# One kernel of attention, gate and routed experts: conversion spread over three engines, unsplit key projections, gathers two units ahead

## Chip, cores, metric

The kernel runs on one core of a Trainium2 chip. The metric is device time in microseconds (us) of one execution, median of several. The engines: PE (TensorE, matmuls), DVE (VectorE), ACT (ScalarE), POOL (GpSimd), SP (SyncE, which issues DMAs here). Each engine works through its own queue in order.

## What is computed

Three stages, one after the other, on 2304 tokens (4 batches of 576), 8 heads of 64, model width 512.

```python
# 1. attention with random features; phi for q and k
proj = einsum('bhsd,df->bhsf', x, w_phi)
proj = proj - max(abs(proj), axis=-1)
phi  = concatenate([exp(proj), exp(-proj)], axis=-1)
kv, z = einsum('bhsf,bhsd->bhfd', k_p, v), sum(k_p, axis=2)
attn = einsum('bhsf,bhfd->bhsd', q_p, kv) / (einsum('bhsf,bhf->bhs', q_p, z) + 1e-6)
# 2. causal convolution of 5 taps as a gate
y = (sigmoid(conv(x, conv_w)) * (x @ w_val)) @ w_out
# 3. per token one of 8 experts: argmax of y @ w_gate,
#    or the one of the token before where sigmoid(y @ w_local) >= 0.5
out[s] = softmax(y @ w_gate)[e] * (relu(y[s] @ w1[e]) @ w2[e])
```

The weights `w_val`, `w_out` and `conv_w` come to the device as 64-bit patterns and are converted to fp32 there.

## The kernel before

The matmuls of weight run in a reduced fp32 format (F32R), three for one product: a number is split into a high part (`hi_of`, a cast) and a low part (`lo_of`, the subtraction), and high x high, high x low and low x high are summed. A full fp32 matmul needs no split.

**Key and query pass** (`run`, L602). 18 tiles of 128 tokens of keys, then 18 of queries, each in two halves of four heads. `load` (L85) brings a raw tile, four buffers; `split` (L104) makes its parts, the cast on ACT and the subtraction on POOL; `proj` (L114) multiplies with the features, with six F32R matmuls for a half tile, or with two fp32 ones where there is no split, as for key tile 0 (L123); DVE then takes the maximum (L131) and subtracts it (L133); ACT makes both exponentials (L136). Three half tiles later `kv` (L147) accumulates keys against values in PSUM, and `kv_done` (L166) copies a batch's sum out. For queries `tq` transposes and `nm` multiplies with that sum.

**Background work.** `from64` (L299) converts a piece of 512 columns of a matrix in six steps: DVE works on the integer pattern (L313, L318, L319, L320, L321, L322), ACT takes an absolute value (L314). Each step is one entry of a queue, `bgq` for the small vector and the four pieces of `w_val`, `bg2` for the four of `w_out`; `setup_w` (L343) adds an entry that begins a piece and one that splits the result, and for `w_out` a fold onto the router's weights. `run` takes 1.3 entries per half tile in the key pass and up to seven in the query pass. A planner that simulates the engines sets the order in which each engine gets its instructions, except where an order is pinned.

**Gate and output.** `conv`, `val` and `lgt_a`/`lgt_b` follow the queries; `ymm` (L522) makes the rows y, 12 F32R matmuls of 512 columns for 128 tokens, and writes them and the expert probabilities to HBM (`y_d`). `yfill(n)` (L412) pins n of these matmuls into PE's queue; the routing (from L675) is a chain of small transposes on PE and steps on DVE, with such fills between, ten of them ahead of the first transpose (L676). After the table (L754) 30 idle matmuls bridge the time until the first rows are gathered (L759).

**Experts.** Ten units: one of two chunks of 128 tokens for each expert, then two of three chunks, whose expert is read at run time. `gather` (L808) fetches rows of y and their probabilities with an indirect DMA of POOL, three buffers; `rows` (L816) transposes and splits them and picks out the probabilities, by a copy (L830) or, in three-chunk units, by three DVE steps (L833 to L835). `unit` (L839) runs the first layer, eight slices of 12 matmuls into `hp` (three buffers), ACT making the high part of the hidden rows (L852) and DVE the remainder `hlo` (L853); then the second layer, chunk by chunk, each scaled by its probability (L867) and scattered by POOL (L868). Behind the first chunk `mid` (L909) calls `rows` for the next unit; that unit's `gather` stands at the beginning of the current one (L899). A loop at the end serves further units; it is empty for these tokens.

Of the kernel before, what the change touches and what calls it, by code (L numbers as in the profile page):

```python
# [8 lines left out]
F32 = mybir.dt.float32  # L9
# [4 lines left out]
AF = mybir.ActivationFunctionType  # L14
# [7 lines left out]
NT = T // 128  # L22
# [7 lines left out]
NCOL = 2 * E + 3 * NUNIT  # L30
YLAG = 4
WARM = 30
FRESH = -1.5 * 2.0 ** -23


@with_exitstack
def body(ctx, tc, qT, kT, v1, wbd, w_val, conv_w, w_out, w_gl, w1, w2, out):
# [65 lines left out]

    def split(nm, t):  # L104

        if t >= NT or (nm, t) in hl_t or (nm, t) == ("k", 0):
            return
        hi = ap.tile([128, 4, 128], F32R, tag="qkh", name="qkh", bufs=2)
        lo = ap.tile([128, 4, 128], F32R, tag="qkl", name="qkl", bufs=2)
        hi_of(A, hi, raw_t[nm, t])  # L110
        lo_of(G, lo, raw_t[nm, t], hi)
        hl_t[nm, t] = (hi, lo)
# [186 lines left out]
    def from64(raw, n, tag):  # L299

        hi = raw[:, :, 1]
        top = raw.bitcast(U16)[:, :, 1]
        if tag == "w":
            slots = (("a", "xh"), ("b", "xh"), ("m", "xl"), ("f", "xl"))
            a, b, m, f = [mp.tile([128, n], I32, tag=w, name=f"t{z}{tag}", bufs=2) for z, w in slots]
        else:
            a, b, m, f = [mp.tile([128, n], I32, tag=f"t{z}{tag}", name=f"t{z}{tag}", bufs=1) for z in "abmf"]
        af, bf, mf, ff = [z.bitcast(F32) for z in (a, b, m, f)]  # L310

        def first():
            V.tensor_scalar(f, hi, 0x07ffffff, 3, op0=ALU.bitwise_and, op1=ALU.logical_shift_left)  # L313
            A.activation(af, hi.bitcast(F32), AF.Abs)  # L314

        return f, [
            first,
            lambda: V.scalar_tensor_tensor(b, hi, -0x40000000, f, ALU.bitwise_and, ALU.bitwise_or),  # L318
            lambda: V.tensor_scalar(m, b, -0x800000, None, op0=ALU.bitwise_and),  # L319
            lambda: V.scalar_tensor_tensor(mf, top, 0.5, mf, ALU.add, ALU.mult),  # L320
            lambda: V.scalar_tensor_tensor(ff, mf, 2.0 ** -36, bf, ALU.mult, ALU.add),  # L321
            lambda: V.scalar_tensor_tensor(ff, af, 2.0 ** -15, ff, ALU.is_ge, ALU.mult),  # L322
        ]

    def setup_small():
        wgl = mp.tile([128, 4, E + 1], F32, name="wgl")
# [85 lines left out]
    def yfill(n):  # L412
        for _ in range(n):
            while rest:
                mm = next(rest[0], None)
                if mm is None:
                    rest.pop(0)
                else:
                    pin(mm)
                    break  # L420
# [252 lines left out]


    tp = pst([NT, 128], "tp1")  # L675
    yfill(10)  # L676
    pin(PE.transpose(tp, rc["code"], ident))
    sc = t_([NT, 128], "sc")
    V.tensor_tensor_scan(sc, rc["onef"][0:NT, :], tp, 0.0, ALU.mult, ALU.max)
# [128 lines left out]
    def gather(gcols):  # L808
        xs = []
        for gc in gcols:  # L810
            xg = fx.tile([128, YW], F32, tag="xg", name="xg", bufs=3)
            G.indirect_dma_start(out=xg, out_offset=None, in_=y_d, in_offset=bass.IndirectOffsetOnAxis(ap=gc, axis=0))
            xs.append(xg)
        return xs

    def rows(xs, probs):  # L816

        xh = fx.tile([128, 4, UNIT], F32R, tag="xh", name="xh")
        xl = fx.tile([128, 4, UNIT], F32R, tag="xl", name="xl")
        pv = []  # L820
        for j, xg in enumerate(xs):
            xp = ps_f.tile([128, 4, 128], F32, tag="xp", name="xp", bufs=2)
            for c in range(4):
                PE.transpose(xp[:, c, :], xg[:, c * 128:(c + 1) * 128], ident)
            sl = slice(j * 128, j * 128 + 128)
            hi_of(A, xh[:, :, sl], xp)
            lo_of(V, xl[:, :, sl], xp, xh[:, :, sl])
            p = fx.tile([128, 1], F32, tag="p", name="p", bufs=6)
            if isinstance(probs, int):
                V.tensor_copy(p, xg[:, D + probs:D + probs + 1])  # L830
            else:
                es = fx.tile([128, E], F32, tag="es", name="es")
                V.tensor_scalar(es, io8, probs, None, op0=ALU.is_equal)  # L833
                V.tensor_tensor(es, es, xg[:, D:YW], ALU.mult)
                V.tensor_reduce(p, es, axis=AX.X, op=ALU.add)  # L835
            pv.append(p)
        return xh, xl, pv

    def unit(hl, x, scols, between, mid):  # L839
        (w1h, w1l), (w2h, w2l) = hl  # L840
        xh, xl, pv = x
        n = len(pv) * 128
        hh = fx.tile([128, 8, UNIT], F32R, tag="hh", name="hh", bufs=1)
        hlo = fx.tile([128, 8, UNIT], F32R, tag="hlo", name="hlo", bufs=1)
        for f in range(8):
            hp = ps_f.tile([128, UNIT], F32, tag="hp", name="hp", bufs=3)
            i = 0
            for k in range(4):
                for wt, xt in ((w1h, xh), (w1l, xh), (w1h, xl)):
                    PE.matmul(hp[:, 0:n], lhsT=wt[:, k, f * 128:(f + 1) * 128], rhs=xt[:, k, 0:n], start=(i == 0), stop=(i == 11))  # L850
                    i += 1
            A.activation(hh[:, f, 0:n], hp[:, 0:n], AF.Relu)  # L852
            V.scalar_tensor_tensor(hlo[:, f, 0:n], hp[:, 0:n], 0.0, hh[:, f, 0:n].bitcast(F32), ALU.max, ALU.subtract)  # L853
            if f % 2 == 1:
                between()
        for j in range(len(pv)):
            op = ps_f.tile([128, 512], F32, tag="op", name="op", bufs=2)
            sl = slice(j * 128, j * 128 + 128)
            i = 0
            for f in range(8):  # L860
                for ht, wt in ((hh, w2h), (hh, w2l), (hlo, w2h)):
                    PE.matmul(op, lhsT=ht[:, f, sl], rhs=wt[:, f, :], start=(i == 0), stop=(i == 23))  # L862
                    i += 1
                if f in (3, 7):
                    between()
            osb = fx.tile([128, 512], F32, tag="osb", name="osb")
            A.activation(osb, op, AF.Copy, scale=pv[j])  # L867
            G.indirect_dma_start(out=out, out_offset=bass.IndirectOffsetOnAxis(ap=scols[j], axis=0), in_=osb, in_offset=None,  # L868
                                 bounds_check=T - 1, oob_is_err=False)
            if j == 0:  # L870
                mid()
# [18 lines left out]
            p()()  # L890
    xs = gather(cols(gidx, units[0][0], units[0][1]))
    cur_x = rows(xs, unit_probs(0))
    for i, (c0, n, e) in enumerate(units):
        last = i + 1 == len(units)
        nxt = {}
        work = []
        if not last:
            nxt["w"], pieces = unit_weights(i + 1)
            nxt["xs"] = gather(cols(gidx, units[i + 1][0], units[i + 1][1]))  # L899
            started = [p() for p in pieces[:3]]  # L900
            todo = pieces[3:]

# [5 lines left out]

        def mid():  # L909
            if not last:  # L910
                nxt["x"] = rows(nxt["xs"], unit_probs(i + 1))

        unit(cur_w, cur_x, cols(sidx, c0, n), between, mid)
        while not last and started:
# [47 lines left out]
```

## Time and profile before

| | us |
|---|---|
| runs of the kernel | 601.49, 601.50, 603.31 (median 601.5) |
| the profiled execution | 600.88, of which the span from first to last instruction 599.2 |
| PE busy | 565.9 (94%) |
| DVE busy | 373.3 (62%) |
| ACT busy | 314.3 (52%) |
| POOL busy | 231.4 (39%) |

Busy time is the union of an engine's instructions; a matmul's end is modelled, so a short pause between matmuls can vanish in it. "Idle before" an instruction is the time in which its engine had nothing running, with the instruction or DMA that ended it. Rows of a time line give the start, the length, engine, line, operation and operands of an instruction or of several alike.

### The profile page before, as it was taken

How to read it: one execution, taken by the hardware profiler on the slowest of the kernel's cores; microseconds unless marked ns; L12 is line 12 of the kernel's file. 1: busy time of each engine (PE TensorE's matmuls, PEld its weight loads, DVE VectorE, ACT ScalarE, POOL GpSimd, SP SyncE). 2: the span in 40 equal slices, each digit the busy share in tenths (PEclk: the TensorE clock that was granted, in tenths of full speed). 3: DMA queues.
4: the chain of work that ended last, by engine and by line, in shares of the span. 5: the costliest groups of instructions: out<-in, count | busy, mean ns of one | idle time of the engine just before them, and what ended most of it. 6: DMA issues, size and time to landing. Idle time of an engine off the chain costs nothing. (4 is left out here: it accounts for less than half of the span.)

```text
span 599.2 us, 13671 instructions
## 1 busy us (share of the span) xinstructions
PE 565.9 (94%) x5545; PEld 497.4 (83%) x5546; DVE 373.3 (62%) x744; ACT 314.3 (52%) x581; POOL 231.4 (39%) x257
## 2 busy tenths in 40 slices
PE   7997998999999999998998999999998989999993
PEld 6886987889888988886775888988987879898982
DVE  6999859688877877478504766666554746460110
ACT  5767855665766655555215565564553646441210
POOL 4454323489878876472204102302302123011001
PEclk9999999999999999999998999999999999999997
DMA  8933422101110001034226877866866648520000
GB/s 278 339 101 124 131 74 59 49 2 37 36 38 2 21 19 38 19 124 139 111 107 200 288 237 254 268 181 189 284 186 203 203 137 276 179 90 35 18 18 35
DMA packets 46017, 76.82 MB, mean 128 GB/s; under 512 B 3839, under 2 KB 22399, under 8 KB 45952
## 3 DMA queue, kind: packets, MB, share of 16 engines
q1 hardware_dynamic: 39840, 60.55, 32.5%
q0 software_dynamic: 3520, 10.58, 4.9%
q10 hardware_dynamic: 2592, 4.79, 2.1%
q8 instruction: 45, 0.74, 0.5%
q14 instruction: 20, 0.16, 0.1%
HBM read 66.39 MB, written 10.56 MB: 128 GB/s over the span
## 5 line engine op out<-in xcount | busy, mean ns | idle before, releaser
L868 POOL DMA_INDIRECT out<-osb,sidx x22 | 28.6, 1302 | 206.7 <-ACT osb L867 161.4
L850 PE MATMUL hp<-xh,w1h 128*128 128x256 f32 (+1 forms) x320 | 94.6, 296 | 7.3 <-DVE hlo L853 5.8
L850 PE MATMUL hp<-xh,w1l 128*128 128x256 f32 (+1 forms) x320 | 94.2, 294 | 0.0
L850 PE MATMUL hp<-xl,w1h 128*128 128x256 f32 (+1 forms) x320 | 93.8, 294 | 0.0
L850 PEld LDWEIGHTS hp<-xh,w1h 128*128 128x128 f32 x320 | 60.8, 190 | 10.4 <-DVE hlo L853 7.1
L862 PE MATMUL op<-w2h,hh 128*128 128x512 f32 x176 | 69.1, 401 | 0.2 <-ACT hh L852 0.2
L51 DVE TENSOR_TENSOR w2l<-wraw,w2h 128x1024 fp32r<-128x1024 f32 x40 | 48.9, 1224 | 32.1 <-ACT w2h L48 22.4
L51 POOL TENSOR_TENSOR qkl<-raw,qkh 128x512 fp32r<-128x512 f32 x35 | 46.7, 1334 | 55.5 <-ACT qkh L48 55.4
L862 PE MATMUL op<-w2l,hh 128*128 128x512 f32 x176 | 67.9, 395 | 0.0
L862 PE MATMUL op<-w2h,hlo 128*128 128x512 f32 x176 | 66.8, 395 | 0.0
L51 DVE TENSOR_TENSOR w1l<-wraw,w1h 128x1024 fp32r<-128x1024 f32 x40 | 48.9, 1250 | 22.6 <-ACT w1h L48 22.6
L131 DVE TENSOR_REDUCE m<-pj 128x4 f32<-128x512 f32 x72 | 49.1, 685 | 22.0 <-PE pj L128 21.9
L265 DVE SCALAR_TENSOR_TENSOR acc<-xT,tfs,acc 128x256 f32<-128x256 f32 (+1 forms) x112 | 53.9, 486 | 13.3 <-ACT acc L263 12.0
L850 PEld LDWEIGHTS hp<-xh,w1l 128*128 128x128 f32 x320 | 60.7, 190 | 1.5
L850 PEld LDWEIGHTS hp<-xl,w1h 128*128 128x128 f32 x320 | 60.5, 189 | 0.0
L48 ACT CAST w2h<-wraw 128x1024 fp32r<-128x1024 f32 x40 | 41.8, 1049 | 34.0 <-DMA wraw<-w 25.2
L853 DVE SCALAR_TENSOR_TENSOR hlo<-hp,hh 128x256 fp32r<-128x256 f32 (+1 forms) x80 | 33.9, 445 | 39.6 <-ACT hh L852 39.5
L852 ACT ACTIVATE hh<-hp 128x256 fp32r<-128x256 f32 (+1 forms) x80 | 31.2, 404 | 48.0 <-PE hp L850 47.6
L48 ACT CAST w1h<-wraw 128x1024 fp32r<-128x1024 f32 x40 | 40.4, 1052 | 29.6 <-DMA wraw<-w 29.6
L133 DVE TENSOR_TENSOR pp<-pj,m 128x512 f32<-128x512 f32 x72 | 48.8, 683 | 2.5 <-PE tp L185 0.8
L158 PE MATMUL kv<-v,ex 128*64 128x65 f32 (+1 forms) x1280 | 46.9, 224 | 3.3 <-DVE kvsb L170 1.4
L158 PEld LDWEIGHTS kv<-v,ex 128*64 128x64 f32 (+1 forms) x1280 | 41.0, 137 | 9.3 <-DVE kvsb L170 1.7
(192 smaller groups left out, 1364.5 us busy)
## 6 DMA issues: line engine op xcount, KB each, us to landing
wraw<-w SPq DMA_DIRECT2D x80, 512.0 KB, 4.5
v<-v SPq DMA_DIRECT2D x18, 260.0 KB, 3.2
y_d<-ysb ACTq DMA_DIRECT2D x18, 260.0 KB, 2.0
raw<-qT SPq DMA_DIRECT2D x18, 256.0 KB, 3.4
raw<-kT SPq DMA_DIRECT2D x17, 256.0 KB, 5.0
wr<-w_val SPq DMA_DIRECT2D x4, 512.0 KB, 7.4
wr<-w_out SPq DMA_DIRECT2D x4, 512.0 KB, 7.6
xg<-y_d,gidx POOLq DMA_INDIRECT x22, 5.4
```

What stands on the lines that cost most here:

```text
L48: (A.copy if eng is A else eng.tensor_copy)(hi, src)
L51: eng.tensor_tensor(lo, src, hi.bitcast(F32), ALU.subtract)
L131: V.tensor_reduce(m, pj, axis=AX.X, op=ALU.max, apply_absolute_value=True)
L133: V.tensor_tensor(pp, pj, m.unsqueeze(2).to_broadcast([128, 4, 128]), ALU.subtract)
L158: PE.matmul(kv_ps[b][blk // 7][mh * 64:mh * 64 + 64, (blk % 7) * VW:(blk % 7 + 1) * VW], lhsT=kp_t[t, hh][off:off + n, sg, h, mh * 64:mh * ...
L265: W["tap"] = V.scalar_tensor_tensor(acc[c], xs, cw[:, kk, c:c + 1], acc[c], ALU.mult, ALU.add)
L850: PE.matmul(hp[:, 0:n], lhsT=wt[:, k, f * 128:(f + 1) * 128], rhs=xt[:, k, 0:n], start=(i == 0), stop=(i == 11))
L852: A.activation(hh[:, f, 0:n], hp[:, 0:n], AF.Relu)
L853: V.scalar_tensor_tensor(hlo[:, f, 0:n], hp[:, 0:n], 0.0, hh[:, f, 0:n].bitcast(F32), ALU.max, ALU.subtract)
L862: PE.matmul(op, lhsT=ht[:, f, sl], rhs=wt[:, f, :], start=(i == 0), stop=(i == 23))
L868: G.indirect_dma_start(out=out, out_offset=bass.IndirectOffsetOnAxis(ap=scols[j], axis=0), in_=osb, in_offset=None, bounds_check=T - 1, oo ...
```

## The change

Four edits. Key tiles are no longer split, and so all go through the fp32 matmuls. The conversion of a piece has four steps in place of six; one operation goes to ACT (a copy with scale and bias, which reads the upper half-word) and two to POOL (a multiplication and an addition), and DVE keeps four. The first fill of the routing has 18 matmuls instead of 10. Gathers have six buffers and are issued two units ahead, in `mid`; the probabilities are taken in `unit`, behind the last remainder of the first layer on DVE.

```diff
+XG = 6
     def split(nm, t):
-        if t >= NT or (nm, t) in hl_t or (nm, t) == ("k", 0):
+        if t >= NT or (nm, t) in hl_t or nm == "k":
             return
...
-        def first():
+        def high():
             V.tensor_scalar(f, hi, 0x07ffffff, 3, op0=ALU.bitwise_and, op1=ALU.logical_shift_left)
             A.activation(af, hi.bitcast(F32), AF.Abs)
-        return f, [
-            first,
-            lambda: V.scalar_tensor_tensor(b, hi, -0x40000000, f, ALU.bitwise_and, ALU.bitwise_or),
-            lambda: V.tensor_scalar(m, b, -0x800000, None, op0=ALU.bitwise_and),
-            lambda: V.scalar_tensor_tensor(mf, top, 0.5, mf, ALU.add, ALU.mult),
-            lambda: V.scalar_tensor_tensor(ff, mf, 2.0 ** -36, bf, ALU.mult, ALU.add),
-            lambda: V.scalar_tensor_tensor(ff, af, 2.0 ** -15, ff, ALU.is_ge, ALU.mult),
-        ]
+        def join():
+            V.scalar_tensor_tensor(b, hi, -0x40000000, f, ALU.bitwise_and, ALU.bitwise_or)
+            A.activation(ff, top, AF.Copy, bias=2.0 ** -37, scale=2.0 ** -36)
+        def low():
+            V.tensor_scalar(m, b, -0x800000, None, op0=ALU.bitwise_and)
+            G.tensor_tensor(mf, ff, mf, ALU.mult)
+            G.tensor_tensor(ff, mf, bf, ALU.add)
+        return f, [high, join, low, lambda: V.scalar_tensor_tensor(ff, af, 2.0 ** -15, ff, ALU.is_ge, ALU.mult)]
...
-    yfill(10)
+    yfill(18)
     pin(PE.transpose(tp, rc["code"], ident))
...
-            xg = fx.tile([128, YW], F32, tag="xg", name="xg", bufs=3)
+            xg = fx.tile([128, YW], F32, tag="xg", name="xg", bufs=XG)
...
-            p = fx.tile([128, 1], F32, tag="p", name="p", bufs=6)
-            if isinstance(probs, int):
-                V.tensor_copy(p, xg[:, D + probs:D + probs + 1])
-            else:
...
-            pv.append(p)
+            pv.append((xg, probs))
+    def prob(xg, probs):
+        p = fx.tile([128, 1], F32, tag="p", name="p", bufs=6)
+        if isinstance(probs, int):
+            V.tensor_copy(p, xg[:, D + probs:D + probs + 1])
+        else:
...
+        return p
...
-            V.scalar_tensor_tensor(hlo[:, f, 0:n], hp[:, 0:n], 0.0, hh[:, f, 0:n].bitcast(F32), ALU.max, ALU.subtract)
+            low = V.scalar_tensor_tensor(hlo[:, f, 0:n], hp[:, 0:n], 0.0, hh[:, f, 0:n].bitcast(F32), ALU.max, ALU.subtract)
             if f % 2 == 1:
                 between()
+        with tc.issue_after(low.ins):
+            pv = [prob(*z) for z in pv]
...
     cur_x = rows(xs, unit_probs(0))
+    xs = {1: gather(cols(gidx, units[1][0], units[1][1]))}
     for i, (c0, n, e) in enumerate(units):
...
-            nxt["xs"] = gather(cols(gidx, units[i + 1][0], units[i + 1][1]))
...
         def mid():
             if not last:
-                nxt["x"] = rows(nxt["xs"], unit_probs(i + 1))
+                nxt["x"] = rows(xs.pop(i + 1), unit_probs(i + 1))
+                if i + 2 < len(units):
+                    xs[i + 2] = gather(cols(gidx, units[i + 2][0], units[i + 2][1]))
```

## Rows read from the trace of the kernel before

**Rows 1.** By stage: from:to, length; PE, PEld, DVE, ACT, POOL; clock, DMA, GB/s.

```profile
20.00:62.00 42.00, 38.13 (x725) 33.33 (x725) 41.34 (x67) 30.58 (x58) 19.66 (x14) 1.00 0.48 157
62.00:91.40 29.40, 29.40 (x590) 26.37 (x586) 19.90 (x30) 19.39 (x37) 9.00 (x7) 1.00 0.35 104
91.40:115.00 23.60, 20.04 (x273) 18.05 (x273) 21.83 (x47) 15.80 (x32) 11.08 (x8) 1.00 0.18 51
115.00:250.00 135.00, 133.77 (x1733) 119.55 (x1731) 98.79 (x250) 82.24 (x187) 102.34 (x119) 1.00 0.08 25
...
452.00:492.00 40.00, 35.02 (x228) 31.61 (x227) 20.82 (x37) 17.81 (x30) 9.55 (x7) 1.00 0.57 181
```

**Rows 2.** Time line of PE, steady key pass: start, length, instruction, count, idle before.

```profile
82.58 0.38 PE L128 MATMUL pj<-wb_hi,qkh 128*128 128x256 f32 x1
82.80 0.28 PE L128 MATMUL pj<-wb_lo,qkh 128*128 128x256 f32 x1
82.92 0.28 PE L128 MATMUL pj<-wb_hi,qkl 128*128 128x256 f32 x1
...
84.57 0.39 PE L128 MATMUL pj<-wb_hi,qkh 128*128 128x256 f32 x1
```

**Rows 3.** Time line of PE at the start: key tile 0 unsplit, then tile 1.

```profile
3.62 3.75 PE L128 MATMUL pj<-wraw,raw 128*128 128x256 f32 x8 [3.62 <-DMA raw<-kT]
...
7.61 0.42 PE L128 MATMUL pj<-wb_hi,qkh 128*128 128x256 f32 x1
7.83 0.41 PE L128 MATMUL pj<-wb_lo,qkh 128*128 128x256 f32 x1
```

**Rows 4.** Groups by line and form: busy us, mean ns; idle before, by whom ended.

```profile
L51 POOL TENSOR_TENSOR qkl<-raw,qkh 128x512 fp32r<-128x512 f32 x35 | 46.7, 1334 | 55.5 <-ACT qkh L48 55.4
...
L320 DVE SCALAR_TENSOR_TENSOR tmw<-wr,tmw 128x512 f32<-128x512 uint16 x8 | 6.8, 855 | 0.0
...
L321 DVE SCALAR_TENSOR_TENSOR tfw<-tmw,tbw 128x512 f32<-128x512 f32 x8 | 5.4, 678 | 0.0
...
L314 ACT ACTIVATE taw<-wr 128x512 f32<-128x512 f32 x8 | 5.4, 671 | 2.1 <-DVE tfw L321 2.1
...
L128 PE MATMUL pj<-wraw,raw 128*128 128x256 f32 x8 | 3.8, 651 | 3.6 <-DMA raw<-kT 3.6
```

**Rows 5.** Time line of PE: last output matmuls and the idle ones, 512 columns.

```profile
311.38 0.39 PE L532 MATMUL yps<-wout_l,gh 128*128 128x512 f32 x1
311.61 0.40 PE L532 MATMUL yps<-wout_h,gl 128*128 128x512 f32 x1
...
312.50 6.64 PE L759 MATMUL idle<-ohl,ones 128*128 128x512 bf16 x29
```

**Rows 6.** Time line of DVE in the key pass.

```profile
23.85 0.68 DVE L133 TENSOR_TENSOR pp<-pj,m 128x512 f32<-128x512 f32 x1
24.45 0.41 DVE L319 TENSOR_SCALAR tmw<-tbw 128x512 int32<-128x512 int32 x1
...
41.61 1.49 DVE L319 TENSOR_SCALAR tmw<-tbw 128x512 int32<-128x512 int32 x1 [0.48 <-POOL wval_l L51]
```

**Rows 7.** Time line of PE: its longest waits from 20 to 62 and 91.4 to 115.

```profile
55.11 1.27 PE L158 MATMUL kv<-v,ex 128*64 128x65 f32 x36 [1.16 <-DVE kvsb L170]
...
102.61 1.15 PE L197 MATMUL num<-kvsb,ex 128*64 128x65 f32 x32 [1.18 <-ACT ex L139]
```

**Rows 8.** Time line of PE: first transpose of the routing.

```profile
282.33 0.28 PE L677 MATMUL tp<-ident,code 128*18 128x128 f32 x1 [1.69 <-DVE code L520]
```

**Rows 9.** Time line of DVE in the last two-chunk unit.

```profile
459.98 0.17 DVE L834 TENSOR_TENSOR es<-es,xg 128x8 f32<-128x8 f32 x1 [4.03 <-DMA xg<-y_d,gidx]
...
461.36 1.08 DVE L853 SCALAR_TENSOR_TENSOR hlo<-hp,hh 128x256 fp32r<-128x256 f32 x3
```

**Rows 10.** Time line of PE, first layer, the waits behind those of rows 9.

```profile
461.83 0.39 PE L850 MATMUL hp<-xh,w1h 128*128 128x256 f32 x1 [2.66 <-DVE hlo L853]
...
488.23 0.38 PE L850 MATMUL hp<-xh,w1h 128*128 128x256 f32 x1 [2.32 <-DVE hlo L853]
```

More of the change, by code (lines that the diff above doesn't have):

```diff
@@ L827, in rows @@
             lo_of(V, xl[:, :, sl], xp, xh[:, :, sl])
-            p = fx.tile([128, 1], F32, tag="p", name="p", bufs=6)
-            if isinstance(probs, int):
-                V.tensor_copy(p, xg[:, D + probs:D + probs + 1])
-            else:
[L832 to L835, printed above, removed]
-            pv.append(p)
-        return xh, xl, pv
+            pv.append((xg, probs))
+        return xh, xl, pv
+    def prob(xg, probs):
[3 more added lines that the diff above has]
+        else:
+            es = fx.tile([128, E], F32, tag="es", name="es")
+            V.tensor_scalar(es, io8, probs, None, op0=ALU.is_equal)
+            V.tensor_tensor(es, es, xg[:, D:YW], ALU.mult)
+            V.tensor_reduce(p, es, axis=AX.X, op=ALU.add)
+        return p
     def unit(hl, x, scols, between, mid):
```

## Prediction

> **What bounds the kernel now.** I read the table by stages first, because the page's 94% for TensorE (PE) is a mean over stages with different limits. In [rows 1] the second column is PE's busy time. From 62 to 91.4 us and from 115 to 250 us PE is idle for at most 1% of the stretch: there only PE's own work counts, and an engine made faster beside it gains nothing. The exceptions are 20 to 62 us (PE 38.13 of 42.00, VectorE, DVE, 41.34), 91.4 to 115 us (PE 20.04 of 23.60, DVE 21.83) and 452 to 492 us (PE 35.02 of 40.00, and DVE only half busy). In the first two PE waits for a saturated DVE; in the last it waits for something that DVE itself waits for. Second I read PE's timeline for the size of one step of the key pass, third DVE's timeline in the three bad stretches for what ended PE's waits.
>
> **Part 1, raw key projections: more work on PE.** In the steady stretch one half tile of keys takes PE 1.99 us, from the projection at 82.58 to the next at 84.57 [rows 2]: six reduced-precision matmuls of 256 columns, 0.12 us apart, then the kv matmuls. The change replaces the six by two full fp32 matmuls. Tile 0 of the keys already runs so: the eight instructions in [rows 3] are four matmuls, so each is two passes, and a half tile needs four passes. They took 3.75 us together; less the last one's length (their mean is 0.65 [rows 4]), that is 3.1 us for seven starts, 0.44 each, while the reduced ones right after start 0.22 apart, not the 0.12 of later on. So PE still ran at half pace there, and a pass costs twice a reduced matmul of the same columns. At full pace no row has one. Bounds: 0.216 us, the spacing of the 512-column bf16 matmuls (6.64 us, less 0.40 for the last one's length as of the 512-column row above it, over 29 intervals, since 30 were issued and one is missing from the record), and 0.24 us, twice 0.12. The 512-column reduced matmuls beside them stand 0.23 apart [rows 5]. I take 0.224, between the two 512-column rows, the nearest kin in streaming time. A half tile then costs 4 x 0.224 = 0.90 in place of 6 x 0.12 = 0.72, that is 0.18 more; 17 tiles have 34 halves, **+6.1 us** (34 x 0.144 = +4.9 to 34 x 0.24 = +8.2). It lies on the path: PE is the bound in the key pass.
>
> [...]
>
> What goes in return: 17 casts on ScalarE (ACT) and 17 subtractions on GpSimd (POOL), 1.33 us each [rows 4]. Neither is the bound. Loads of raw tiles now wait for the projection and not for the split, with four buffers and loads three tiles ahead: about 12 us of lead at two half tiles of 2 us each. I cost that at nothing; if SyncE's queue stood still behind such a load, the later key and value tiles queued behind it would come late too, and PE would wait.
>
> **Part 2, the conversion of the two weight matrices.** Eight pieces of 512 columns. DVE loses two of its six operations (855 and 678 ns), ACT gains one copy (its Abs of the same size took 671 ns), POOL gains two two-input operations (1.33 us each by its subtraction) [rows 4]. DVE starts one such operation every 0.60 us [rows 6], so the eight pieces give back 16 x 0.60 = 9.6 us of DVE, and up to 12.3 by durations. POOL gets 16 x 1.33 = 21.3 us and loses 17 x 1.33 = 22.6. Fewer steps also mean fewer pops of the background queue: a value piece took 8 and takes 6, an output piece 9 and now 7 with its fold. At 1.3 pops a half tile over 36 half tiles there are some 45: before, 6 + 4 x 8 = 38 went to the small vector and value pieces and 7 were left for the output matrix; after, 4 + 4 x 6 = 28 go there and 17 are left, two and a half output pieces. So most of what DVE converts in the stretch from 91.4 to 115 us moves into the key pass.
>
> What it is worth is PE's idle time in the two DVE-bound stretches. From 20 to 62 us it is 42.00 - 38.13 = 3.87 us [rows 1]; the largest single wait is for DVE's late kvsb copy, 1.16 us at 55.11 [rows 7]. DVE's load per half tile falls to two operations at 0.60 plus some 0.4 of conversion (1.9 us a piece in 4.6 half tiles), well under the 2.17 us that PE will need. Next late is then PE itself, and the swap of the kv accumulators between batches stays. I take **-3.4** (-2.0 to -3.9). From 91.4 to 115 us it is 3.56 us, for instance 1.18 us at 102.61 [rows 7]. With one and a half pieces in place of three the DVE stretch is no longer full; I take **-2.6** (-1.0 to -3.6). PE's transposes and folds of the output pieces move with them and cost the same.
>
> The change adds waits: ACT's copy overwrites what DVE's second operation reads, so ACT waits for DVE; POOL waits for both; DVE's last operation waits for POOL. Behind the last one on DVE stand the reduce and subtract of later half tiles, for which ACT's exponentials and PE's kv wait. This is the first rival.
>
> **Part 3, 18 fills instead of 10 ahead of the first routing transpose.** PE stands idle 1.69 us at 282.33 until DVE's code is there [rows 8]; eight more output matmuls at 0.23 [rows 5] are 1.84 us of work that is needed anyway and stands now behind the routing. They fit the hole: **-1.7** (0 to -1.7). The last output rows, for which the gather waits, then land that much earlier.
>
> **Part 4, gathers two units ahead and probabilities behind the first layer.** At 459.98 DVE sits idle 4.03 us in the middle of a unit: its next instruction multiplies the gathered probabilities, and the gather has not landed. A second such wait follows. Only then the three hidden remainders behind it (hlo, 461.36) are made [rows 9], and PE, which has no free accumulator, resumes at 461.83 after 2.66 us; so again at 488.23 after 2.32 [rows 10]. Both holes belong to the gathers for the two three-chunk units, which had three buffers between them; the row has their probability steps queued ahead of the running unit's remainders. With six buffers and an issue one unit earlier (some 22 us) the rows lie there long before; and the probabilities stand behind the last hlo, so that nothing of that layer is queued behind them. Moved with them: the gathers pass, on POOL's queue, from the start of a unit to behind its first scatter; the scatters of later chunks stand behind them, at about 1 us an issue, and nothing but the end of the program waits for those. In starts instead of idle ends each hole is some 0.15 longer: **-5.3** (-4.0 to -5.5).
>
> **Sum.** The profiled execution took 600.9 us (span 599.2). +6.1 - 3.4 - 2.6 - 1.7 - 5.3 = -6.9, so 594.0; the median of the runs is 0.6 above the profiled one, so **594.6**. All ends against it: +8.2 - 2.0 - 1.0 - 0 - 4.0 = +1.2 (602.7); all for it: +4.9 - 3.9 - 3.6 - 1.7 - 5.5 = -9.8, and about 2 us more from the refill of PE's pipeline after some 15 to 20 short waits: 589.7.
>
> **Rivals.**
> *The round trip over POOL stops DVE (slower).* Place: DVE's last operation of a piece, in the key pass. If it is queued directly behind its own chain, DVE stands for two POOL operations and the ACT copy, 2 x 1.33 + 0.67 = 3.3, with handovers about 3.9 us a piece. A piece comes every 6/1.3 = 4.6 half tiles, 10 us of PE; DVE needs 4.6 x 1.2 = 5.5 for keys and 1.9 for the piece, so the spare is 2.6 us. Above that it decides: 1.3 us too much over seven pieces is 9 us, and the 3.4 of the key pass is not gained. 594.6 + 9 + 3.4 = 607. For it: DVE runs in order and already waited for POOL once, at 41.61 [rows 6]. Against it: key work stands between the conversion's operations there, so the queue need not stop. Chance 0.08.
> *The stall behind the hidden layer keeps its length*, because DVE is late for other reasons (weight remainders of the next unit queue there too): 594.6 + 5.3 = 599.9. Against it: the idle time is DVE's own, and the row names the gather. Chance 0.06.
> *Raw weight loads are not hidden at full pace.* A load of 128 stationary columns fits into the 0.12 us between two reduced matmuls [rows 2], so it is at most that long. If it stood bare before each pass: 4 x 0.12 x 34 = 16 us more, 611. Against it: at half pace the passes of [rows 3] start two reduced spacings apart and no more, which leaves no room for a bare load. Chance 0.03.
> That the longer fill does nothing would give 596.3 and lies inside the range.
>
> **How the numbers follow.** The forecast holds 0.83 with its bounds 589.7 to 602.7, of which little lies above 599.7. The range of 589 to 601 leaves out the first and third rival and the outer ends. A measurement here tells 0.3% (1.8 us) from no change: faster 0.80, same 0.09 (mostly the second rival), slower 0.11.
>
> **What would show it.** Right: in the key pass raw passes 0.22 apart and a steady half tile of 2.15 to 2.2 us; no PE idle above 1 us between 20 and 62 us beyond batch swaps; no wait at the first routing transpose; no wait for a gather on DVE after the first unit, and no PE gap above 1 us around the three-chunk units. Wrong: DVE idle ended by a POOL operation of the conversion; raw passes above 0.25; PE waiting for raw tiles; a hole of two microseconds still before one of the three-chunk units.

## The result, and the profile after

The changed kernel takes **596.9 us** (median; 594.06 to 598.66 in four runs) against 602.4 for the kernel before in the same measurement: a ratio of **0.989**, 95% interval 0.986 to 0.993, or 5.6 us less. The forecast was 594.6 with a range of 589 to 601. The profiled execution took 596.0 us, span 594.2, against 600.9 and 599.2.

The line numbers are some four higher than before. Marks worked out from the two time lines of PE (us): first kv matmul, end of the key pass, first routing transpose, end of the output matmuls, first expert matmul, last matmul's end.

| | kv | keys end | routing | outputs end | experts | end |
|---|---|---|---|---|---|---|
| before | 10.46 | 91.45 | 282.33 | 311.85 | 323.14 | 589.70 |
| after | 12.02 | 94.97 | 285.50 | 313.18 | 325.89 | 584.36 |

So the front half became 1.3 us longer, the handover to the experts another 1.4 longer, and the experts 8.1 shorter (266.56 to 258.47). By stage, to be held against [rows 1] (from:to, length, then busy time of PE, PEld, DVE, ACT, POOL, then clock, DMA share, GB/s):

```profile
20.00:62.00 42.00, 38.96 (x676) 30.62 (x675) 35.37 (x57) 29.93 (x54) 17.75 (x14) 1.00 0.51 148
62.00:94.90 32.90, 32.85 (x586) 26.93 (x584) 25.65 (x37) 21.43 (x39) 12.27 (x9) 1.00 0.35 99
94.90:117.00 22.10, 21.69 (x279) 20.08 (x275) 14.76 (x30) 11.80 (x26) 9.91 (x8) 0.92 0.17 49
117.00:250.00 133.00, 131.73 (x1656) 116.48 (x1656) 99.90 (x251) 81.90 (x183) 102.82 (x120) 1.00 0.10 30
323.00:331.00 8.00, 6.23 (x28) 5.70 (x29) 6.05 (x7) 4.45 (x8) 4.55 (x4) 0.57 0.90 325
452.00:492.00 40.00, 40.00 (x256) 36.15 (x255) 23.44 (x36) 20.69 (x33) 10.79 (x7) 1.00 0.59 191
```

DVE is no longer full in the first of these stretches (35.37 of 42.00, before 41.34) nor in the third (14.76 of 22.10). The hole of the last row is gone: PE is busy for all 40 us. New are the clock column in the third row (0.92) and the fifth row (0.57): stretches at half clock, a granted clock of 0.50. Before, there was one such stretch while PE worked, 3.41 us at the start of the experts (from 323.49). In both traces the clock falls to 0.50 once more behind the last matmul, for the last 6.1 us before and 7.6 after.

PE's time line of the steady key pass, as [rows 2], and of the start, as [rows 3]:

```profile
79.02 1.13 PE L129 MATMUL pj<-wraw,raw 128*128 128x256 f32 x4
80.08 1.15 PE L159 MATMUL kv<-v,ex 128*64 128x65 f32 x32
81.17 0.48 PE L129 MATMUL pj<-wraw,raw 128*128 128x256 f32 x1
...
3.61 8.48 PE L129 MATMUL pj<-wraw,raw 128*128 128x256 f32 x24 [3.61 <-DMA raw<-kT]
```

A half tile is now 2.15 us (79.02 to 81.17), 0.16 more than the 1.99 before. Four passes fill 1.13 us, the last of them 0.48 as the row of one; (1.13 - 0.48) / 3 is **0.216 us** between passes at full pace.

Groups by line and form, the conversion's operations (as [rows 4]), and two of DVE's waits in its time line:

```profile
L326 DVE SCALAR_TENSOR_TENSOR tfw<-taw,tfw 128x512 f32<-128x512 f32 x8 | 6.3, 782 | 5.0 <-POOL tfw L324 5.0
...
L323 POOL TENSOR_TENSOR tmw<-tfw,tmw 128x512 f32<-128x512 f32 x8 | 10.2, 1277 | 34.5 <-DVE tmw L322 28.9 <-ACT ex L139 5.0 <-ACT ex L140 0.6
L324 POOL TENSOR_TENSOR tfw<-tmw,tbw 128x512 f32<-128x512 f32 x8 | 10.2, 1273 | 0.6
...
20.68 0.69 DVE L326 SCALAR_TENSOR_TENSOR tfw<-taw,tfw 128x512 f32<-128x512 f32 x1 [1.42 <-POOL tfw L324]
...
41.85 0.69 DVE L326 SCALAR_TENSOR_TENSOR tfw<-taw,tfw 128x512 f32<-128x512 f32 x1 [1.47 <-POOL tfw L324]
```

So DVE does stand for POOL's round trip, five times, 5.0 us in all, 1.5 at most. PE's own waits of the key pass that are left are the swaps of the batches (time line of PE; [rows 7] before), and the wait of [rows 8] is gone, with an output matmul right behind the transpose:

```profile
32.80 1.03 PE L159 MATMUL kv<-v,ex 64*64 64x65 f32 x28 [0.60 <-ACT kvsb L171]
34.59 1.59 PE L159 MATMUL kv<-v,ex 64*64 64x65 f32 x42 [0.76 <-DVE kvsb L171]
...
54.92 0.34 PE L159 MATMUL kv<-v,ex 128*64 128x65 f32 x4 [0.62 <-DVE kvsb L171]
...
285.26 0.40 PE L535 MATMUL yps<-wout_h,gl 128*128 128x512 f32 x1
285.50 0.27 PE L680 MATMUL tp<-ident,code 128*18 128x128 f32 x1
285.52 0.48 PE L535 MATMUL yps<-wout_h,gh 128*128 128x512 f32 x1
```

The handover to the experts, POOL's and PE's time line:

```profile
318.31 1.20 POOL L815 DMA_INDIRECT xg<-y_d,gidx  x1 [10.23 <-DMA y_d<-ysb]
320.76 0.94 POOL L815 DMA_INDIRECT xg<-y_d,gidx  x1 [1.24 <-PE idle L762]
...
324.10 1.12 PE L827 MATMUL xp<-ident,xg 128*128 128x128 f32 x4 [1.47 <-DMA xg<-y_d,gidx]
325.89 0.58 PE L857 MATMUL hp<-xh,w1h 128*128 128x256 f32 x1 [0.68 <-ACT xh L49]
```

The second gather stands 1.24 us for the idle matmuls: one of the six buffers lies over memory that these still read. PE gets its first expert matmul 5.41 us behind the last idle one, 4.00 before, and the low stretch around it, at a clock of 0.50, lasts 6.83 us (from 323.84) instead of 3.41.

In the experts, the two longest waits of PE that are left, and what ACT did ahead of the second (time lines of PE and ACT; [rows 10] before):

```profile
366.57 0.39 PE L857 MATMUL hp<-xh,w1h 128*128 128x256 f32 x1 [0.77 <-DVE hlo L860]
381.44 0.50 PE L871 MATMUL op<-w2h,hh 128*128 128x512 f32 x1 [0.93 <-ACT hh L859]
...
380.06 1.05 ACT L49 CAST w2h<-wraw 128x1024 fp32r<-128x1024 f32 x1 [3.27 <-DMA wraw<-w]
381.01 0.38 ACT L859 ACTIVATE hh<-hp 128x256 fp32r<-128x256 f32 x1
```

The hidden part `hh` stood in ACT's queue behind a cast of the next unit's weights that waited for its DMA. DVE waits for no gather any more behind the first unit; before that was 14.9 us in six waits.

### The profile page after: what moved, and what is told of

Its sections match the earlier page's. It is cut to its first block, busy times and chain, and to the rows that moved or that the text cites. A ratio compares the mean times of both kernels' runs of the same rounds, so it can differ in the third digit from the quotient of the medians.

```text
span 594.2 us, 13524 instructions
## 1 busy us (share of the span) xinstructions
PE 569.9 (96%) x5477; PEld 495.5 (83%) x5478; DVE 365.2 (61%) x726; ACT 313.1 (53%) x573; POOL 238.0 (40%) x258
## 5 line engine op out<-in xcount | busy, mean ns | idle before, releaser
L815 POOL DMA_INDIRECT xg<-y_d,gidx x22 | 36.7, 1669 | 98.5 <-DVE p L838 83.4
```

## The experiments

Twelve versions, each beside the kernel before. Besides the ratio I use one worked-out number, **full-clock length**: span times mean granted clock, averaged over a version's runs. It is an estimate of what the span would be if PE had been the bound in every stretch at a clock of 0.50 and had had 1.00 there. It takes the clock's part out of a difference, roughly, since waits in these stretches are scaled like work; the stretches behind the last matmul (6.1 and 7.6 us in the two profiles) are in it as well. The profile gives the clock as a share of full speed: where an expectation names a frequency, what was measured is 0.50, and no run shows the frequency. The runs of one version scatter in it by 0.9 to 2.6 us (standard deviation), so that a row of the table holds to 1 to 2 us, and the difference of two rows to about 2. For the kernel before it is 593.0 to 593.5 in the three measurements that list its clocks, for the changed one 585.6, here held against 593.1. Mean clocks are 0.987 and 0.985.

| version | ratio, 95% interval | median us | full-clock, against before |
|---|---|---|---|
| changed kernel | 0.989 [0.986, 0.993] | 596.9 | -7.5 |
| raw_alone | 1.015 [1.012, 1.018] | 611.1 | +4.5 |
| conversion_alone | 1.006 [1.003, 1.009] | 606.1 | +0.1 |
| gathers_alone | 0.989 [0.987, 0.992] | 596.8 | -6.3 |
| gathers_ahead_alone | 0.997 [0.995, 0.999] | 600.2 | -3.3 |
| probabilities_alone | 1.065 [1.062, 1.068] | 642.7 | +21.9 |
| all_but_raw | 0.986 [0.983, 0.989] | 594.1 | -10.5 |
| all_but_conversion | 0.992 [0.989, 0.995] | 598.0 | -5.5 |
| all_but_filler | 0.997 [0.994, 0.999] | 599.8 | -5.3 |
| all_but_gathers | 1.005 [1.001, 1.008] | 605.1 | -0.3 |
| gathers_and_filler | 0.987 [0.984, 0.990] | 594.3 | -8.3 |
| idle_on_identity | 0.992 [0.989, 0.995] | 597.5 | -6.5 |
| all_but_raw_idle_on_identity | 0.986 [0.982, 0.989] | 593.5 | -8.5 |

**Raw keys alone**, on the kernel before:

```diff
-        if t >= NT or (nm, t) in hl_t or (nm, t) == ("k", 0):
+        if t >= NT or (nm, t) in hl_t or nm == "k":
```

> The kernel before with unsplit key projections alone. Theory: TensorE is the bound of the key pass, so the whole of the dearer passes shows, 34 half tiles x (4 x 0.216 - 6 x 0.12) = 34 x 0.144 = 4.9 us, less about 1 us of waits that the subtraction on GpSimd ended: +3.5 to +5 us, ratio 1.006 to 1.008. Rival: between 20 and 62 us the projections are hidden under a saturated VectorE, so only the other half of the tiles shows: +1.5 to +2.5 us, ratio 1.0025 to 1.004.

Measured 1.015, more than either theory. But the key pass ends only 2.1 us later (93.56 against 91.45), and 1.6 of that is the later first kv (12.10 against 10.46). From there to the end of the pass it takes 81.46 us, before 80.98, although a half tile takes 0.16 us longer: part of the longer projections fell into time in which PE had waited, for its idle time from 20 to 62 us falls from 3.87 to 1.87 us. More is lost later. PE's and ACT's time lines in the experts:

```profile
363.81 0.50 PE L862 MATMUL op<-w2h,hh 128*128 128x512 f32 x1 [2.82 <-ACT hh L852]
...
362.43 1.04 ACT L48 CAST w2h<-wraw 128x1024 fp32r<-128x1024 f32 x1 [1.13 <-DMA wraw<-w]
363.38 0.65 ACT L852 ACTIVATE hh<-hp 128x256 fp32r<-128x256 f32 x2
...
518.90 0.39 PE L850 MATMUL hp<-xh,w1h 128*128 128x256 f32 x1 [1.99 <-DVE hlo L853]
```

No instruction of the experts was edited, and yet there is a hole of a kind that the kernel before had not, behind an ACT queue that waits for weights, and one of the old kind at another unit. In this execution, 3 us shorter than the median, the experts took 268.91 us (327.83 to 596.74), 2.4 more than before; 2.1 us were lost from 91 to 283 us, where PE ran at half clock from 105.0 us for 3.41 (0.51 from 105.0 to 108.4). PE's idle time in the experts is not longer than before (7.06 us against 7.96), but they have 10.24 us at half clock in place of 3.41: 6.83 at their start and 3.41 behind the hole at 363.81. Of the 4.5 us at full clock this one profile shows the 2.1 of the key pass; where the rest lies isn't shown.

**The conversion alone**, on the kernel before (the whole conversion hunk of the change):

```diff
-            lambda: V.scalar_tensor_tensor(mf, top, 0.5, mf, ALU.add, ALU.mult),
-            lambda: V.scalar_tensor_tensor(ff, mf, 2.0 ** -36, bf, ALU.mult, ALU.add),
...
+            A.activation(ff, top, AF.Copy, bias=2.0 ** -37, scale=2.0 ** -36)
...
+            G.tensor_tensor(mf, ff, mf, ALU.mult)
+            G.tensor_tensor(ff, mf, bf, ALU.add)
```

> The kernel before with the conversion on three engines alone. Theory: VectorE gets 9.6 us back and TensorE's idle time from 20 to 62 and 91 to 115 us falls from 7.4 to about 3 us: -3.5 to -5 us, ratio 0.992 to 0.994. Rival: the last step waits on VectorE for GpSimd, which also has the keys' subtractions here: 0 or slower, ratio 1.000 to 1.005, and VectorE rows that GpSimd's product or sum ended.

The number is about the rival's (1.006, and 1.005 at most there). Its mechanism is there in small: DVE stands for POOL's sum four times, 1.6 us in all, but the output matmuls end only 0.4 us later than before (312.26). The experts lose the rest (270.60 us, 323.55 to 594.15; 266.56 before): one hole is in the same unit as before, the other a unit later, and each is now followed by 3.4 us at half clock (PE's time line, then stretches as in [rows 1]), which in the profile of before they were not (1.00 from 450 to 550 us):

```profile
463.48 0.39 PE L852 MATMUL hp<-xh,w1h 128*128 128x256 f32 x1 [2.42 <-DVE hlo L855]
...
514.79 0.38 PE L852 MATMUL hp<-xh,w1h 128*128 128x256 f32 x1 [2.38 <-DVE hlo L855]
...
464.80:468.20 3.40, 3.40 (x12) 2.72 (x11) 2.17 (x3) 2.98 (x5) 0.00 (x0) 0.50 0.00 0
516.00:519.40 3.40, 3.40 (x12) 2.82 (x11) 1.65 (x3) 2.57 (x4) 0.00 (x0) 0.50 0.00 0
```

What PE waits for in the key pass says what the conversion could give there (PE's waits from 20 to 62 us: in all, times, longest; first before, then with the conversion alone):

```profile
PE kv L158 <- DVE kvsb L170: 1.4, 2, 1.2
...
PE kv L158 <- ACT kvsb L170: 0.7, 1, 0.7
...
PE kv L158 <- DVE kvsb L170: 1.6, 2, 0.9
PE kv L158 <- ACT kvsb L170: 1.5, 1, 1.5
```

Before, 2.0 of the 3.87 us are swaps of the accumulator, which wait for a copy (`kvsb`). With the conversion alone all other waits are gone, but the swaps take 3.1 us, all that is left.

**The fourth part alone**, on the kernel before (the hunks of `gather`, `rows`, `prob`, `unit` and the loop):

```diff
+XG = 6
...
+        with tc.issue_after(low.ins):
+            pv = [prob(*z) for z in pv]
...
+                    xs[i + 2] = gather(cols(gidx, units[i + 2][0], units[i + 2][1]))
```

> The kernel before with the fourth part alone: six gather buffers, gathers two units ahead, probabilities behind the first layer. Theory: both holes of the last two-chunk unit and the first three-chunk unit close (-6 us over these two units), but the experts' start comes later as in the changed kernel, since the second gather waits for the end of the idle matmuls whose tile its new buffer overlies (+2 to +3 us): net -3 to -4 us, ratio 0.9935 to 0.995. Rival: the late start comes from elsewhere (the other parts' order of instructions): net -6 us, ratio 0.990.

0.989: this part alone gives the whole gain of the change; the other three together add nothing that these runs can tell. The number is the rival's, but the late start of the experts is in it too, as the theory had it (5.12 us between idle and expert matmuls, 6.83 at half clock), so it belongs to this part, and the holes were worth more than the theory gave.

**All but the raw keys**: the changed kernel with the first diff above turned round.

> The changed kernel with the keys split again as before (tile 0 unsplit). Theory: raw projections cost and the other parts do not need them: 4 to 5 us faster than the changed kernel, ratio to the kernel before 0.980 to 0.983. Rival: GpSimd then has the 17 subtractions of the keys and the 16 new operations, 44 us in a key pass of 80 us, and VectorE's last step of a piece comes late: no faster than the changed kernel, ratio 0.988 to 0.992.

0.986, between the two: beside the other parts raw keys cost 2.0 us by the medians' ratios (0.989 - 0.986) and 3.0 at full clock. This execution had 6.83 us at half clock in the key pass, behind a wait of 1.06 us, with PE busy throughout (stretches as in [rows 1]):

```profile
20.00:32.70 12.70, 11.64 (x229) 10.36 (x229) 11.98 (x19) 11.78 (x24) 9.96 (x7) 1.00 0.81 269
32.70:39.50 6.80, 6.80 (x100) 6.34 (x99) 3.32 (x7) 3.37 (x7) 3.88 (x3) 0.50 0.33 100
```

**The two halves of the fourth part.** Gathers ahead alone has the first and third lines of the diff of the fourth part, with the probabilities in `rows` as before; probabilities alone has the second, with three buffers and the gathers at the start of the unit.

> The kernel before, with six buffers and the gathers issued two units ahead alone; the probabilities stay with the transposes of the rows. Theory one: with the rows there in time the probabilities cost VectorE little (under 1 us for a unit of three chunks), so the holes close by this alone, less the later start of the experts (about 1.4 us and 3.4 us at 1.2 GHz): 4 to 6 us gained, ratio 0.990 to 0.993, like both halves together (0.989). Theory two: both halves are needed: a gain of under 2.5 us, ratio 0.996 to 1.000, with DVE still behind hlo at the second layer.

> The kernel before, with the probabilities alone moved behind the first layer of their unit; the gathers stay at the start of the unit before, with three buffers. Theory one: what holds VectorE in the units with the holes is the reduction over the gathered row of a late gather, so moving it closes most of the holes: the units that took 26.45 and 25.90 us take 23 to 24, and the time falls by 3 to 5 us, ratio 0.992 to 0.995. Theory two: the late gather holds the transposes of the rows on PE and the low halves on VectorE just as long, so the move alone gains under 1.5 us: 0.998 to 1.002, with the holes at the next unit's transposes.

Gathers ahead alone: 0.997, half of the gain: both halves are needed for all of it. DVE still stands for a gather ahead of three `hlo`, less often (two waits in place of six), the longer of them 5.21 us (DVE's and PE's time line):

```profile
416.46 0.17 DVE L835 TENSOR_TENSOR es<-es,xg 128x8 f32<-128x8 f32 x1 [5.21 <-DMA xg<-y_d,gidx]
416.54 1.08 DVE L854 SCALAR_TENSOR_TENSOR hlo<-hp,hh 128x256 fp32r<-128x256 f32 x3
...
417.02 0.38 PE L851 MATMUL hp<-xh,w1h 128*128 128x256 f32 x1 [1.85 <-DVE hlo L854]
```

Probabilities alone: 1.065, 40 us slower, which no theory had. POOL's waits and PE's time line say why:

```profile
POOL xg L812 <- DVE p L835: 123.7, 8, 26.5
...
387.54 0.88 PE L824 MATMUL xp<-ident,xg 128*128 128x128 f32 x4 [2.79 <-DMA xg<-y_d,gidx]
415.90 0.87 PE L824 MATMUL xp<-ident,xg 128*128 128x128 f32 x3 [3.18 <-DMA xg<-y_d,gidx]
...
387.70:391.20 3.50, 3.50 (x18) 3.50 (x18) 2.46 (x4) 2.48 (x3) 0.44 (x1) 0.51 0.96 334
```

The gathered rows are held until the probability is taken, now a unit later, and with three buffers the next gather waits for that (123.7 us on POOL in eight waits). PE's transposes then wait for the landing, 24.3 us in twelve waits, and behind the two waits shown PE runs at half clock: 0.51 from 387.7 to 391.2 us, as above, and 0.51 from 415 to 422. Of the 40 us, 21.9 are at full clock and about 18 are the clock's (0.960 on average). So more buffers are not an extra of the move: with three, and the gathers one unit ahead, it is a loss. Six buffers without the earlier issue were not tried.

**Idle matmuls on the identity**, in the changed kernel, and the same without raw keys:

```diff
-    for _ in range(WARM):
-        pin(PE.matmul(idle, lhsT=rc["ones"], rhs=ohl[:, 0:4, :].rearrange("p t c -> p (t c)"), start=True, stop=True))
+    idb = ident.bitcast(BF16)
+    for _ in range(2 * WARM):
+        pin(PE.matmul(idle[:, 0:256], lhsT=idb[:, 0:128], rhs=idb, start=True, stop=True))
```

> The changed kernel, with one edit: the filler matmuls before the experts read the identity tile (60 of 256 columns) in place of the ones and one-hot tiles (30 of 512 columns), so that the memory of these tiles is free sooner. [...] Theory one: the enlarged pool of gathered rows lies over the tiles that the filler reads, and that alone delays the start: filler end to first expert matmul falls to about 4.0, the low stretch to 3.41, and the time by 2.5 to 3.5 us, ratio to before 0.983 to 0.987 (the changed kernel itself 0.989). Rival: the start is bound by the landing of the gathered rows whatever the filler reads: 5.0 to 5.4 us, ratio 0.988 to 0.991. Second rival: the delay is shorter but the clock stretch stays at 6.83: a gain of 1.2 to 1.4 us, 0.987.

> The changed kernel with the key projections split as before, and the filler matmuls on the identity tile: the two edits that the first runs point to, together. If they add: the version without raw keys measured 0.986 (594.1 us), less 2.5 to 3.5 us of the start of the experts: 590.5 to 592 us, ratio 0.980 to 0.983. If the start is bound by the landing of the rows, it equals the version without raw keys: 0.985 to 0.987.

0.992 and 0.986: no gain in either. The wait of 1.24 us did go, but the start did not come earlier: 6.71 us lie between the last idle and the first expert matmul (time lines of SP, POOL and PE):

```profile
316.77 15.57 SPq L802 DMA_DIRECT2D wraw<-w  x6
...
317.27 1.68 POOL L816 DMA_INDIRECT xg<-y_d,gidx  x1 [9.86 <-DVE w2l L52]
...
323.51 1.11 PE L828 MATMUL xp<-ident,xg 128*128 128x128 f32 x4 [3.62 <-DMA xg<-y_d,gidx]
```

With the memory free, SP issues the next unit's weights too, at 316.77 and not at 322.90 as in the changed kernel, half a microsecond ahead of the first gather. Its rows reach PE 6.2 us after the issue, 3.7 in the changed kernel (318.31 to its first transpose at 321.97). The landing of the rows bounds the start. Without raw keys the first gather (314.18) stands ahead of the weights (314.59) and its rows are at PE after 4.9 us; those of the second (315.94), behind them, after 6.6. So the landing was longer both times that the weights had been issued first; that their traffic is the cause wasn't tested by holding them back.

**Leave-one-out.** The changed kernel without the conversion hunk, without the fourth part, and with `yfill(10)`; and the kernel before with the fourth part and `yfill(18)`.

> The changed kernel with the conversion of the numerators back on VectorE. What the conversion is worth beside the other parts is this time less that of the changed kernel (596.9 us). Theory one (the prediction's terms): 3.4 + 2.6 us, so 602 to 603.5 us, ratio to before 1.000 to 1.003. Theory two (read from the two versions run so far that differ by conversion and filler alone: 596.8 with the fourth part alone, 594.1 with conversion and filler added, of which the filler has 1.7): the conversion is worth about 1 us, because the cuts in the stalls go into TensorE at 1.2 GHz elsewhere: 597.5 to 599, ratio 0.991 to 0.995.

> The changed kernel with ten filler matmuls ahead of the transpose of the codes, as before, in place of eighteen. Theory: TensorE waits 1.5 to 1.8 us for VectorE's code again and all behind it is later by that: 598.3 to 598.8 us, ratio 0.993 to 0.995 (changed kernel 0.989 to 0.992). Rival: the eight fillers only filled time that the y writes and gathers set in any case, so nothing is lost: 596.5 to 597.2, ratio 0.989 to 0.992, with a shorter wait for the gathered rows at the start of the experts.

> The changed kernel with the fourth part undone: gathers and probabilities as before. If the parts add as they do in the leave-one-out runs, the time is the changed kernel's plus 5.3 to 6.5 us: 602 to 603.5 us, ratio 0.999 to 1.002. If the expert stage of before loses more whenever the front half is changed (raw keys alone lost 4.4 us there, the conversion alone 4), the experts take 270 us or more from the first expert matmul to the end instead of 266.6 (changed kernel: 258.5), with holes of over 2 us behind VectorE's hlo or ACT's hh, and the time is 606 to 612 us, ratio 1.006 to 1.016.

> The kernel before with the fourth part and the eighteen fillers alone: keys split, conversion as before. If the conversion is worth about 1 us: 594.5 to 596 us, ratio 0.987 to 0.990. If it is worth the 6 us that the prediction gave it: this is 6 us behind the version with conversion, fourth part and filler (594.1): 599 to 600.5 us, ratio 0.994 to 0.997.

Conversion: worth 1.7 us beside the other parts by the ratios (0.992 - 0.989), and 0.5 beside the fourth part and the filler (0.987 - 0.986); both are inside the intervals. At full clock it is 2.0 and 2.1, each give or take about 2. The time is in theory two's range; its reason, that the gain is lost again to the clock, is not shown, since at full clock the conversion is worth little more.

Filler: 0.997 without it, so it is worth 4.4 us by the ratios, more than expected; in the other pair (gathers_alone, gathers_and_filler) 1.5. At full clock it is 2.1 and 2.0. The wait comes back as [rows 8] had it:

```profile
283.59 0.28 PE L680 MATMUL tp<-ident,code 128*18 128x128 f32 x1 [1.69 <-DVE code L523]
```

The rest of the 4.4 lies in the mean clock (0.983 against 0.985) and within the intervals; the rival, that the eight fillers gain nothing, falls.

Fourth part: 1.005 without it, 9.2 us worse by the ratios, 7.2 at full clock; alone it was 6.3. Between the two expected ranges, and the expectation named 4.4 us for raw keys alone in the experts where the marks give 2.4. The experts took 267.96 us (322.46 to 590.42), less than the 270 of the second theory, with one hole where it was and two elsewhere:

```profile
356.02 0.50 PE L865 MATMUL op<-w2h,hh 128*128 128x512 f32 x1 [2.18 <-ACT hh L855]
462.85 0.39 PE L853 MATMUL hp<-xh,w1h 128*128 128x256 f32 x1 [1.54 <-DVE hlo L856]
512.75 0.39 PE L853 MATMUL hp<-xh,w1h 128*128 128x256 f32 x1 [1.81 <-DVE hlo L856]
```

No version is shown to beat the changed kernel by more than the intervals allow. The best medians, 593.5 to 594.3, are the three without raw keys that have the fourth part and the filler, and the plainest of them, gathers_and_filler, leaves the conversion out as well.

## Why the prediction was right

The time and the sign came out inside the range, 2.3 us above the forecast; but the sum is better than its terms. Raw keys were made 3 us too dear, the conversion 4 us too good and the fourth part 2 us too poor (the last about as much as these numbers scatter), which nearly cancel. That the sum came out so close is luck; that the fourth part carries the gain, and how, was foreseen.

| term | forecast | measured, full clock, with twice the standard error: beside the other parts; alone |
|---|---|---|
| raw keys | +6.1 | +3.0 ± 2.3; +4.5 ± 1.1 |
| conversion | -3.4 - 2.6 | -2.0 ± 1.8; +0.1 ± 1.1 |
| filler | -1.7 | -2.1 ± 1.4; -2.0 ± 1.7 (beside the fourth part) |
| fourth part | -5.3 | -7.2 ± 1.4; -6.3 ± 1.6 |
| sum | -6.9 | -7.5 ± 1.1 for all; -5.6 with the clock |

**Raw keys.** The pass is 0.216 us in the trace, (1.13 - 0.48) / 3, the lower bound, and not 0.224: the nearest kin was the bf16 row, not the reduced one. By that the term is 34 x 0.144 = +4.9. The step that failed is "it lies on the path": in the stretch where DVE was the bound, PE had time for longer projections (its idle time from 20 to 62 us fell from 3.87 to 1.87 in raw_alone). The pass from first kv to its end grew by 0.5 us in raw_alone. What was not costed is the start: tiles 1 and 2 are projected while PE still runs at half pace (passes 0.43 us apart until 9.7 us), and kv begins 1.6 us later. At full clock raw keys cost 3.0 to 4.5 us all the same; start and pass are 2.1 of it, and the place of the rest isn't shown.

**Conversion.** DVE lost 6 us of work between 20 and 62 us, as worked out, and yet PE's idle time there fell only from 3.87 to 3.04 us beside raw keys, and to 3.10 without them. The step that failed is that nearly all of this idle time comes of DVE's load. 2.0 us of it are the swaps of the accumulator, the 1.16 us of [rows 7] among them, and they stay with DVE far from full: 2.2 us in the changed kernel (32.80, 34.59, 54.92 and a short one), 3.1 with the conversion alone. Why the copies still come late isn't shown. The other 1.8 us could be won but once: the conversion alone ends them, and raw keys alone leave 0.3 of them. In sum the two edits were forecast at +2.7 for start and key pass (6.1 - 3.4) and gave +3.5, of which the output pieces' transposes that moved in are part. Behind the key pass the gain was there: PE's idle time in the stretch that follows falls from 3.56 us to 0.41 (22.10 - 21.69 in the third row), somewhat more than the forecast's 2.6. In the profiled execution it was partly given back at once: PE ran at half clock from 108.8 us for 3.41 us, which takes up to 1.7 us from it, as an estimate (half of 3.41). This term named no clock.

**The first rival** was right that DVE would stand for POOL: 5.0 us in five waits. It was wrong on the price, 1.0 us for each of the five and not 3.9, since key work stood between. PE waits 0.8 us behind the first of them, for ACT's exponentials (0.62 at 25.29, 0.18 at 25.81): DVE works without a break from 20.68 on until it has their input, and ACT's new copy stands ahead of them as well. Behind the others PE waits for swaps alone.

**Filler.** As forecast; the hole of 1.69 us was filled.

**The other rivals** did not come about: no stall behind the hidden layer is left around the three-chunk units, and passes 0.216 us apart leave no room for a bare weight load.

**Fourth part.** Both holes are closed as said, and the units that had them fell from 26.45 and 25.90 us to 22.97 and 23.26: 6.1 us. They are the sixth and seventh of the eight two-chunk units (445.08 to 471.53 and on to 497.43), not the last one that [rows 9] names: the probability steps for which DVE stood there belong to a unit that begins at 520.99, and in the changed kernel they run in that unit, from 536.2. "Six buffers" was costed at nothing, and has a price: the handover is 1.4 us longer, with 3.4 us more at half clock around its end. Of the versions with six buffers, the changed kernel and gathers_alone have a handover of 5.41 and 5.12 us, with 6.83 at half clock; of those with three, the kernel before has 4.00 and 3.41, but raw_alone has 6.83 at half clock too. That the buffers lie over tiles still in use is one cause of the wait of the second gather, but ending that wait alone won nothing. That the probabilities need more than three buffers, and that gathers ahead alone gives 2.4 us (602.6 to 600.2), was not in the forecast.

**The signs named.** All of those for right are there: a half tile of 2.15 us, no wait of PE above 0.76 us between 20 and 62 us, none at the routing's transpose, none of DVE for a gather, and no gap of 1 us around the three-chunk units. One of those for wrong is there as well, DVE's idle time ended by POOL; it was the sign of a loss of 0.8 us at most here, because DVE had slack (busy for 35.37 of 42.00 us from 20 to 62). The 2 us for the refill of PE's pipeline, in the lower end of the range, are shown by no row and no run, and were not needed.

**Terms that don't add.** The forecast added four terms. Alone, by the medians, raw keys, conversion and the fourth part come to +8.7, +3.7 and -5.6 us; with the filler's 1.5 that is +5.3 and not -5.6. Most of the difference lies in the experts: with the old order of gathers each edit in the front half, raw keys or conversion, came with holes there that moved, or that were followed by half clock. In each of the two, DVE waits for gathers six times behind the first unit (12.0 and 15.7 us in all). In all seven versions with the whole fourth part, and in the changed kernel, it never does behind the first unit, and there the same edits cost little. That the fourth part removes these waits is shown; why a hole was followed by a fall of the clock in one execution and not in another isn't.

## What to carry to other kernels

Before idle time is booked as a gain, ask of each wait what ends it: more than half of it here were waits for one copy, which stayed when the full engine was relieved. And two edits that draw on the same idle time must be costed together: the one that fills PE's waits and the one that removes them cannot both be booked in full. Where an instruction waits for a DMA ahead of others in an in-order queue, free the queue first, since until then any change elsewhere may move the hole; and count the buffers that a later use holds, because the same move was 6 us better with six buffers and gathers two units ahead, and 40 worse with three and one unit. More buffers may lie over something still in use, here for a wait of 1.24 us: look who last reads that memory, and what else is let loose when it comes free.

## What the runs showed of the hardware

A full fp32 matmul of 256 columns is two passes of 0.216 us at full pace, 0.43 for the pair, against three reduced ones of 0.12.

At the start of the changed kernel these passes start 0.43 us apart until 9.7 us and 0.216 behind it, although the profile's clock column reads 1.00 from 5 to 10 us: the half pace shows in the spacing alone.

PE's clock fell to 0.50 behind short waits, as from 32.7 us in all_but_raw, behind one of 1.06 us, and where PE was busy without a gap: in all_but_raw at 107.8 us, with PE busy for 7.80 of 7.80 us ahead of it, and in the changed kernel at 108.8 us, with PE busy for 6.00 of 6.00 us from 104 to 110. The latter fall lies near the end of 32 matmuls of 9 columns, with others between (104.08 to 109.27). The kernel before has the same 32 from 112.76 to 117.90, with PE busy throughout, and its clock stayed at 1.00. While PE works, the stretches of these two kernels' profiles last 3.41 or 6.83 us. In the long one the expert matmuls start 0.21 us apart (326.27, 326.48, ...) and 0.12 behind it, so 6.83 us at half clock with PE busy would cost about 3, as an estimate.

The mean granted clock differs between versions: 0.987 before, 0.981 with the conversion alone, 0.980 with raw keys alone, 0.960 with the probabilities alone. Of the 3.7 us that the conversion alone lost, all but 0.1 (give or take 1.1) is the clock's by the full-clock length.
